# Talking-heads attention and a Fourier/FFN block on one core: moving the mixing stage's q, k and v loads to other steps

## The chip, the core and the metric

The kernel runs on one core of a Trainium2 chip. The metric is device time in microseconds (us) of one execution. Before the change the median of three runs is 2313.41 us (2312.7 to 2314.76). The profiled execution, from which every duration below is taken, is a separate one: it took 2319.37 us, and its first to last instruction span 2317.0 us.

The engines are named as in the profile: PE (matrix multiply), PEld (its weight load), DVE (vector), ACT (scalar), POOL (GpSimd), SP (the queue that issues most DMAs here). POOL computes and also issues DMAs; while it issues one, the rest of its queue waits.

## The reference, cut to what matters

```python
# q, k, v: (8 batches, 12 heads, 448, 64) fp32
scores = scale * np.matmul(q, k.transpose(0, 1, 3, 2))
scores = np.einsum('bhij,hg->bgij', scores, w_pre)      # mix the heads
attn = np.exp(scores - np.max(scores, axis=-1, keepdims=True))
attn = attn / (np.sum(attn, axis=-1, keepdims=True) + 1e-09)
attn = np.einsum('bhij,hg->bgij', attn, w_post)         # mix them again
x = np.matmul(attn, v)          # then (B, H, S, D) -> (B, S, H*D) = (8, 448, 768)
mixed = np.real(np.fft.fft(np.fft.fft(x, axis=1), axis=2))
u = x + mixed                   # then a layer norm over the last axis: un
ch = np.maximum(un @ w_ch1, 0.0) @ w_ch2                # 768 -> 3072 -> 768
out = u + ch
```

All of it is fp32.

## The kernel before, in words

There are two stages. `mix_phase` does the attention and the Fourier transform, batch after batch, and writes `u` to DRAM; `ffn_phase` does the norm and the two large products, with Strassen-like combinations of blocks. The change is in the first stage, which fills about the first 815 us of the profile.

**Steps.** The mixing stage is one software pipeline of 184 steps, 23 per batch (`GS`), and one step is about 4 us. A batch's 448 query rows are cut into 8 blocks of 2 or 3 steps (`BLOCKS`); a step handles 20 query rows of all 12 heads, laid out so that a small matrix product mixes the heads. For step T the work is spread over earlier steps: the block's q·k products (L628) are copied by ACT from PSUM to a tile `Sb` (L489, two buffers); at the end of step T-5 SP issues four gathers `Kr<-Sb` (L645, 105 KB each), which bring the rows of the 12 heads together; in step T-2 PE does the head mix `mx` (L656), DVE the row maximum (L663), ACT the exponential into `PP` (L670), and POOL divides by the row sums (L680, two instructions); in step T PE does the second head mix `po` (L690) and DVE transposes it (L703). The product with v (L720) comes after each group of two blocks.

A block's copy into `Sb` may not begin before the gathers of the block two before it have landed, because they read the same buffer. That is the wait `ACT Sb L489 <- DMA Kr<-Sb`.

**What else the steps carry.** Around this, each step carries work of the batch before or after: the transposes of the next batch's q and k (L601), the Fourier folds of the batch before on POOL (L785, L790, L799, L800, L806), its transforms on PE (L764, L829, L845), the sums `X` on DVE (L856, L858), the stores of `u` (L877 on SP, an indirect one at L868 and L874 on POOL), and one instruction per step of the preparation of the FFN's weights on DVE (L250 to L310), with its loads and stores on POOL (L234, L243).

**The order** is written by hand. Each piece of work has a due step (`due(kind, at, fn)`), and in every step `take` issues what is due. Pieces of kind "none", the loads among them, are issued first in their step. Within the step the engines' order follows `ORDERS`, of which there is one for even and one for odd steps; because a batch has 23 steps, a given step of a batch is even in one batch and odd in the next. PE, DVE, ACT and POOL execute in exactly the order written.

**The loads of q and k.** A batch needs six tiles, q and k for each of three groups of heads (`xx` = 0, 1, 2). They take turns in four buffers (`praw`). A tile is loaded in two halves (`y` = 0, 1), each half by two DMAs of 112 KB, and for all batches but the first POOL issues them (L572). The tiles are loaded in the order of their transposes, q0, k0, q2, q1, k2, k1, whose steps `AT_T` gives: 5, 9, 13, 15, 15 and 16 of the batch before. `AT_L` gives the steps in which the two halves of each of the six are issued, counted from the start of the batch before (so -4 is step 19 of the batch before that one); `AT_L1` is the same for batch 1. `AT_V` gives the steps for the two halves of the three v tiles, one DMA of 224 KB each (L581), counted in the batch that uses them; a v tile has one buffer, and its first half waits for the last product that reads the old one (steps 1, 3 and 4).

**The loads and the folds.** The two are tied together. `take` counts the halves of q and k that it issued, and after the scaling of a step

```python
if s < TOT - 3:
    for _ in range(min(len(folds), 1 if n and s > 3 else 2)):
        folds.pop(0)()
```

so one fold piece is issued in a step with such a load and two in a step without. Eight pieces become ready in step 0 of the next batch (popped from step 1), and twelve in its step 6 (popped from step 7). They come in the order pairs, pairs, sides, quarters for each of two combinations; the second list ends with four `both`. The transforms of step 16 (L829) need all of them.

Of the kernel before, what the change touches and what calls it, by code (L numbers as in the profile page):

```python
# [86 lines left out]


AT_T = ((5, 9), (15, 16), (13, 15))
AT_L = ((-4, -3), (-2, -1), (0, 1), (2, 7), (10, 11), (12, 13))  # L90
AT_V = ((2, 3), (4, 5), (6, 7))
AT_L1 = ((-12, -12), (-12, -12), (3, 4), (5, 6), (10, 11), (12, 13))
AT_QK0 = {2: (0, 1, 1), 3: (2, 3, 3), 4: (4, 5, 5)}
AT_QK = ((0, 2, 1), (0, 1, 2), (0, 1, 2), (1, 2, 2),
         (0, 1, 2), (0, 1, 2), (0, 1, 2), (0, 1, 2))
# [355 lines left out]
def mix_phase(ctx, tc, rest, ident, q, k, v, w_pre, w_post, u_scr, u_rev, wts, lead):  # L451
# [125 lines left out]
    def emit_load_v(b, pr, y):  # L577
        if y == 0:
            batches[b]["v", pr] = pvv.tile([P, 2, C7 * D], F32, name="vv", tag=f"vv{pr}")
        h = 6 * y + 2 * pr  # L580
        (nc.gpsimd if b else nc.sync).dma_start(  # L581
            out=batches[b]["v", pr][64 * y:64 * y + 64, :, :],
            in_=v[b, h:h + 2].rearrange("h (p c) d -> p h (c d)", c=C7))
# [301 lines left out]
    def due(kind, at, fn):  # L885
        fill[kind].append((at, len(fill[kind]), fn))
# [4 lines left out]
    for b in range(B):  # L891
# [14 lines left out]
        else:  # L906
            for at, (a, nm, xx) in zip(AT_L if b > 1 else AT_L1, sorted(at_t, key=lambda e: e[0])):
                for y in range(2):
# [6 lines left out]
        for pr in range(3 if b else 0):  # L915
            for y in range(2):
                due("none", f + AT_V[pr][y], lambda b=b, pr=pr, y=y: emit_load_v(b, pr, y))
        for n in range(0 if b else 2, NBL):
# [635 lines left out]
```

## Time and profile before

| | before |
|---|---|
| median of three runs | 2313.41 us |
| profiled execution: its own time / its span | 2319.37 / 2317.0 us |
| PE busy | 2260.0 us, 98% |
| DVE / ACT / POOL busy | 1719.4 / 1167.7 / 1292.1 us |
| mixing stage | up to about 815 us |
| batches 1 to 6 of it, each from its step 0 to the next one's | 93.4, 99.9, 99.3, 98.3, 100.7, 96.7 us |

Busy time of POOL takes in the DMAs that it issues; SP's issues are no busy time. A batch's start is read from the trace as the start of the first head-mix product (L656) of its step 0: 129.7, 223.1, 323.0, 422.3, 520.6, 621.3 and 718.0 us for batches 1 to 7. The start of any other step is read in the same way. Batches 2 to 6 do the same work, and batch 1 lacks only the last transforms of a batch two before it; so differences between them are waits. In the timeline a row is a run of like instructions: start, length, engine, line, tiles, count, and in brackets the idle time before it and what ended that.

### The profile page before, as it was taken

The numbers are of one execution on the slowest core, as the hardware profiler recorded it, in microseconds if no ns is written. First come the engines' busy times: TensorE is split into PE (matmuls) and PEld (weight loads), VectorE is DVE, ScalarE is ACT, GpSimd is POOL, SyncE is SP. The second block draws the span as 40 slices with busy tenths as digits, with TensorE's granted clock in tenths as the row PEclk, the third lists the DMA queues.
The fourth block names the chain that finished last, engine by engine and source line by source line (L and its number), as shares of the span: only waits on it lengthen the run. The fifth ranks groups of instructions, "written<-read, shape, count | busy, mean of one in ns | idle before, by whom it ended". The sixth has DMA issues, their size and how long they took to land.

```text
span 2317.0 us, 60784 instructions
## 1 busy us (share of the span) xinstructions
PE 2260.0 (98%) x22894; PEld 1743.0 (75%) x22894; DVE 1719.4 (74%) x3640; ACT 1167.7 (50%) x3330; POOL 1292.1 (56%) x1799
## 2 busy tenths in 40 slices
PE   7999999999999999999999999999999999999998
PEld 3455555555555577677899999999999999999998
DVE  4778778887877757787777787778777877865545
ACT  4776767666676632322354444444444445434434
POOL 5587968778787552121545465556545645444334
PEclk9999999999999999999999999999999999999999
DMA  7565655657666466567777887879877977795664
GB/s 167 163 185 165 184 168 163 193 157 187 181 178 194 139 233 217 187 218 271 204 180 211 202 239 204 207 178 261 212 168 197 287 169 183 194 246 124 146 147 76
DMA packets 228542, 439.44 MB, mean 190 GB/s; under 512 B 35964, under 2 KB 150326, under 8 KB 228252
## 3 DMA queue, kind: packets, MB, share of 16 engines
q1 hardware_dynamic: 157484, 302.90, 38.6%
q0 software_dynamic: 68480, 131.62, 30.5%
q8 instruction: 183, 3.00, 0.6%
q10 hardware_dynamic: 2288, 1.05, 0.2%
q14 instruction: 107, 0.88, 0.1%
HBM read 213.16 MB, written 143.16 MB: 154 GB/s over the span
## 4 chain that ended last, share of the span: by engine, by line
PE 88%; DVE 5%; DMA 3%; ACT 2%; issue 1%; POOL 1%; SPq 1%; DVEq 0%; ACTq 0%; POOLq 0%
PE psP L1213 18%; PE psP L1335 14%; PE psR L1213 9%; PE psR L1335 7%; PE mx L656 6%; PE ms L720 6%; PE ms L628 5%; PE po L690 5%; PE psQ L1213 4%; PE psQ L1335 3%; PE psP L1290 3%; PE ms L845 2%; PE ms L601 2%; DMA Kr<-Sb 1%; PE psR L1290 1%; PE ms L829 1%
## 5 line engine op out<-in xcount | busy, mean ns | idle before, releaser
L1369 POOL DMA_DIRECT2D out_dram<-od x172 | 208.9, 1277 | 262.6 <-DVE od L1357 171.9
L680 POOL TENSOR_SCALAR PP<-PP,rcp 128x448 f32<-128x448 f32 x368 | 235.3, 649 | 186.9 <-DVE rcp L678 144.0
L670 ACT ACTIVATE PP<-mx,nmx 128x448 f32<-128x448 f32 x368 | 230.2, 631 | 174.0 <-DVE nmx L663 155.7
L663 DVE TENSOR_REDUCE nmx<-mx 128x1 f32<-128x448 f32 x368 | 212.5, 617 | 103.9 <-PE mx L656 101.7
L1176 POOL TENSOR_TENSOR hq<-h 128x128 f32<-128x128 f32 (+1 forms) x210 | 130.0, 619 | 255.4 <-ACT h L1235 122.1
L1363 ACT COPY od<-psP 128x192 f32<-128x192 f32 x488 | 156.1, 320 | 172.4 <-PE psP L1335 171.0
L1366 DVE TENSOR_TENSOR od<-od 128x768 f32<-128x768 f32 x210 | 201.4, 972 | 52.8 <-ACT od L1363 52.4
L489 ACT COPY Sb<-ms 124x448 f32<-124x448 f32 (+1 forms) x378 | 181.7, 540 | 54.0 <-PE ms L628 23.5
L703 DVE STREAM_TRANSPOSE Pv<-po 128x896 f32<-128x896 f32 x184 | 203.5, 1106 | 4.6 <-PE po L690 3.7
L656 PE MATMUL mx<-Kr,kw 60*32 60x448 f32 x2944 | 199.0, 555 | 7.4 <-DMA Kr<-Sb 4.2
L628 PE MATMUL ms<-kT,qT 64*32 64x448 f32 (+1 forms) x3072 | 195.4, 544 | 9.0 <-ACT Sb L489 3.6
L720 PEld LDWEIGHTS ms<-Pv,vv 64*64 64x64 f32 x5376 | 137.9, 132 | 76.7 <-issue 46.4
L690 PE MATMUL po<-PP,kw 60*32 60x448 f32 x2944 | 187.8, 539 | 1.4 <-POOL PP L680 0.8
L1213 PE MATMUL psP<-qs,w1t 128*128 128x256 f32 x744 | 179.2, 379 | 1.4 <-DVE h L1234 1.4
L1213 PE MATMUL psP<-ks,w1t 128*128 128x256 f32 x744 | 179.2, 379 | 0.4 <-DVE h L1234 0.4
L720 PE MATMUL ms<-Pv,vv 64*64 64x120 f32 (+1 forms) x5376 | 160.7, 263 | 6.6 <-ACT Sb L489 3.5
L254 POOL TENSOR_SCALAR wst<-wst 128x256 f32<-128x256 f32 (+1 forms) x76 | 119.2, 1577 | 67.7 <-ACT wst L265 67.6
L1213 PEld LDWEIGHTS psP<-qs,w1t 128*128 128x128 f32 x744 | 139.3, 190 | 18.5 <-DVE h L1234 1.8
L1213 PEld LDWEIGHTS psP<-ks,w1t 128*128 128x128 f32 x744 | 139.3, 190 | 17.4 <-DVE h L1234 0.8
L1213 PE MATMUL psP<-ub,w1t 128*128 128x256 f32 x528 | 127.1, 379 | 0.3 <-DVE h L1234 0.3
L1234 DVE TENSOR_TENSOR h<-h,psP 128x512 f32<-128x512 f32 x42 | 28.8, 686 | 127.8 <-PE psP L1213 112.3
L1335 PE MATMUL psP<-w2t,hq 128*128 128x192 f32 x490 | 122.4, 332 | 1.2 <-DVE od L1357 1.2
(199 smaller groups left out, 5310.2 us busy)
## 6 DMA issues: line engine op xcount, KB each, us to landing
Kr<-Sb SPq DMA_DIRECT2D x730, 105.0 KB
out_dram<-od POOLq DMA_DIRECT2D x172, 384.0 KB, 6.6
qs<-ub SPq DMA_DIRECT2D x89, 384.0 KB
ks<-ub SPq DMA_DIRECT2D x88, 384.0 KB
ub<-ub SPq DMA_DIRECT2D x79, 384.0 KB
w1t<-w SPq DMA_DIRECT2D x42, 384.0 KB
w2t<-w SPq DMA_DIRECT2D x42, 384.0 KB
raw<-in_moe_w_ch_dram SPq DMA_DIRECT2D x32, 384.0 KB
```

The lines of the kernel that those rows point to most:

```text
L628: nc.tensor.matmul(pss[x][o:o + hi - lo, :S], st["qT", xx][64 * x:64 * x + 64, y, lo:hi], st["kT", xx][64 * x:64 * x + 64, y, :], start=Tr ...
L656: nc.tensor.matmul(mx[x][64 * z + o:64 * z + o + 32, :S], kw1[64 * x:64 * x + KR, o:o + 32], Kr[64 * x:64 * x + KR, z, :], start=True, sto ...
L663: nc.vector.tensor_reduce(nmx[:, :], steps[T]["mx"][x][:, :S], axis=AX.X, op=ALU.max, negate=True)
L670: nc.scalar.activation(steps[T]["PP"][:, x, :], steps[T]["mx"][x][:, :S], ACTF.Exp, bias=steps[T]["nmx", x][:, :], accum_out=steps[T]["den ...
L680: nc.gpsimd.tensor_scalar(PP[:, x, :], PP[:, x, :], rcp[:, x:x + 1], 1.0, op0=ALU.mult, op1=ALU.mult)
L690: nc.tensor.matmul(po[o:o + 32, z, :S], kw2[64 * z:64 * z + KR, y, :], PP[64 * z:64 * z + KR, :, c * HS:(c + 1) * HS], start=True, stop=True)
L703: nc.vector.transpose(turned[a]["Pv"][:, j, :].rearrange("p (z s) -> p z s", z=2), steps[T]["po"][:, :, :S])
L720: nc.tensor.matmul(pss[y][64 * x:64 * x + 64, :nu * R], st["v", pr][64 * y:64 * y + 64, x, jb * D:(jb + 1) * D], _ap(Pv, 64 * y * rp + 32 ...
L1213: mm = nc.tensor.matmul(p[:, m, :], w1[i][:, kc, m * P:(m + 1) * P], ub[:, kc, :], start=i in (0, 4, 1)[:3 - seed] and m == kc == 0, stop= ...
L1335: nc.tensor.matmul(ps[j, key][:, :DQ], a, b, start=m in (0, 4), stop=True, skip_group_check=True)
L1366: eng.tensor_tensor(D[j][:, :, :], D[j][:, :, :], D[k][:, :, :], op=ALU.add)
L1369: nc.gpsimd.dma_start(out=acc[t, r, d], in_=D[j][:, :, :], accum_op=ALU.add)
```

## The change

Three constants change. For batches 2 to 7 the first four tiles of q and k (q0, k0, q2, q1) are issued one half per step in steps 15 to 22 of the batch two before, where they were spread over steps 19 to 22 and then 0, 1, 2 and 7; k2 is issued in steps 8 and 9, where it was in 10 and 11; k1 stays in 12 and 13. For batch 1 three of its tiles are one or two steps sooner, within batch 0. Of v, the second half of the second tile goes from step 5 to 4, and the third tile from 6 and 7 to 5 and 6.

```diff
 AT_T = ((5, 9), (15, 16), (13, 15))
-AT_L = ((-4, -3), (-2, -1), (0, 1), (2, 7), (10, 11), (12, 13))
-AT_V = ((2, 3), (4, 5), (6, 7))
-AT_L1 = ((-12, -12), (-12, -12), (3, 4), (5, 6), (10, 11), (12, 13))
+AT_L = ((-8, -7), (-6, -5), (-4, -3), (-2, -1), (8, 9), (12, 13))
+AT_V = ((2, 3), (4, 4), (5, 6))
+AT_L1 = ((-12, -12), (-12, -12), (2, 3), (4, 5), (8, 9), (12, 13))
```

No instruction is added or taken away. The order on PE, DVE, ACT and SP is the same as before; on POOL the DMA issues and, through the rule above, the fold pieces stand elsewhere.

## The prediction

> **What bounds the kernel now.** I read the page's busy times first, then busy times by stretches of steps, then waits and timelines inside the stretches that are too long. PE is busy nearly throughout, so only its waits can be won or added:
>
> ```profile
> span 2317.0 us, 60784 instructions
> PE 2260.0 (98%) x22894; PEld 1743.0 (75%) x22894; DVE 1719.4 (74%) x3640; ACT 1167.7 (50%) x3330; POOL 1292.1 (56%) x1799
> ```
>
> PE is idle for 57 us of the whole span. The next view is the busy time in steps 0 to 3 of batches 2 to 6, one row each (the columns are named in the first line):
>
> ```profile
> core 0: us, PE busy (x) PEld busy (x) DVE busy (x) ACT busy (x) POOL busy (x), PEclk, DMA share, GB/s
> 223.10:243.10 20.00, 18.34 (x347) 9.84 (x343) 14.73 (x35) 11.60 (x38) 13.56 (x19) 1.00 0.74 207
> 323.00:344.80 21.80, 20.09 (x352) 10.55 (x348) 15.15 (x38) 12.06 (x41) 14.71 (x22) 0.92 0.82 215
> 422.30:440.60 18.30, 18.30 (x350) 10.23 (x350) 14.71 (x35) 11.59 (x38) 13.52 (x19) 1.00 0.81 217
> 520.60:542.80 22.20, 19.67 (x350) 10.45 (x346) 15.42 (x38) 12.19 (x41) 14.20 (x21) 0.92 0.82 192
> 621.30:639.10 17.80, 17.48 (x353) 9.72 (x352) 15.18 (x35) 11.65 (x37) 14.95 (x21) 1.00 0.77 207
> ```
>
> The same work takes 17.8 to 22.2 us. With the shortest as floor the excess is 100.1 - 5 x 17.8 = 11.1 us. The modelled ends of matmuls hide part of a wait in busy time, so I count lengths, not gaps. The same view of steps 15 to 18 gives 19.0, 16.9, 17.7, 17.3 and 16.8 us at a DMA share of 0.32 to 0.50: excess 87.7 - 5 x 16.8 = 3.7 us. Steps 19 to 22 take 16.7 us in all five batches: excess 0, with two q or k DMAs in every step. Steps 4 to 14, of which two batches stand here, give 44.2, 43.9, 45.6, 44.5 and 45.4 us, excess 223.6 - 5 x 43.9 = 4.1 us:
>
> ```profile
> 344.80:388.70 43.90, 43.44 (x972) 23.03 (x957) 35.79 (x71) 32.94 (x102) 43.05 (x67) 1.00 0.60 177
> 440.60:486.20 45.60, 44.02 (x964) 23.28 (x969) 38.37 (x75) 33.10 (x108) 44.12 (x68) 1.00 0.66 194
> ```
>
> Here POOL is the second full engine: 43.05 of 43.90 us and 44.12 of 45.60. So there are two different shortages, of DMA in steps 0 to 3 and of POOL in steps 4 to 14; in all 18.9 us.
>
> The timeline of batch 5, step 2, shows the first:
>
> ```profile
> 532.03 1.42 POOL L572 DMA_DIRECT2D rawq<-in_q_dram  x2
> 532.95 0.97 ACT L489 COPY Sb<-ms 124x448 f32<-124x448 f32 x2 [3.48 <-DMA Kr<-Sb]
> 533.54 1.41 PE L628 MATMUL ms<-kT,qT 64*32 64x448 f32 x16 [1.85 <-ACT Sb L489]
> ```
>
> ACT may not overwrite `Sb` until SP's gathers have landed, and PE waits for ACT. The gathers are late because the DMA engines are full: the q loads issued beside them take twice as long as in steps 19 to 22. The tile view of rawq, first for 520.6 to 536 us, then for 604.6 to 621 us:
>
> ```profile
> DMA to landing us min/median/max: 8.4/8.5/8.7
> ```
>
> ```profile
> DMA to landing us min/median/max: 4.4/4.4/4.4
> ```
>
> For the gathers I worked landings out of the trace's semaphore records (last record before the semaphore's next use). The slowest of a step's four takes a median of 7.0 to 7.3 us when issued in steps 0 to 2, and 2.4 to 3.4 us in 15 to 18. In step 0 it is 8.9, 8.0, 6.6, 8.8 and 4.3 us in batches 2 to 6; the long batches are those above 8.
>
> POOL's timeline, batch 4, shows the second shortage, an unbroken row:
>
> ```profile
> 471.96 1.49 POOL L572 DMA_DIRECT2D rawk<-in_k_dram  x2
> 473.49 1.25 POOL L680 TENSOR_SCALAR PP<-PP,rcp 128x448 f32<-128x448 f32 x2
> 474.71 0.99 POOL L785 TENSOR_TENSOR xs<-X 113x384 f32<-113x384 f32 x1
> 475.66 1.43 POOL L572 DMA_DIRECT2D rawk<-in_k_dram  x2
> ```
>
> There the scaling of `PP` ends 0.06 to 0.6 us before PE's `po` needs it in most of steps 8 to 15, against 4 us in steps 17 to 21 (worked out from the trace).
>
> **What the Trainium skill says.** "DMA: Bandwidth & Descriptors", section "SWDGE vs HWDGE vs iDMA": DMAs from POOL and from SP use the same DMA engines, which take turns between their queues. The landings above agree: loads on POOL and gathers on SP are slow together. The same page, "Anatomy of one DMA", fits 2.0 us plus bytes at 436 GB/s, an estimate of 2.3 us for 112 KB alone; the fastest q or k load of the trace took 2.9 us, so 8.5 us is mostly queueing. "SBUF — State Buffer", "SBUF: two separate sides": a POOL instruction and a DVE one that needs the second port exclude each other whole. The trace agrees: in batch 2, step 15, `tmp<-wst` (L289) took 3.06 us in place of 0.27 us while POOL ran without a pause, and PE then waited 1.05 us for DVE's `kT`.
>
> **The change part by part.**
>
> *q2 and the first half of q1 leave steps 0, 1 and 2.* That is 3 halves x 2 DMAs = 6. Their DMA cost from the windows: 19 to 22 (8 such DMAs, mean share 0.53) less 15 to 18 (none, mean 0.39) is 0.14 x 16.7 us / 8 = 0.29 us of all engines each; from packet times (one of 256 ns and one of 134 ns per engine) 0.39 us. So 6 x 0.29 to 0.39 = 1.7 to 2.3 us leave some 13 us, and the share there falls from about 0.8 to 0.62-0.67. v's loads, the stores of `u` and the weights stay. Steps 4 to 8 have a share of 0.7 and gathers of 4.2 to 4.7 us (6.7 in step 8), so I expect about 5 us, under the 6.6 that cost batch 4 little. I take two thirds of the 11.1 us: **-7.4 us**. Bounds: 0 if the rest keeps it full, -11.1 if all goes.
>
> *POOL in steps 0 to 15.* One issue is 0.722 us (tile rows). Eight leave steps 0 to 7 (5.8 us). The folds, with a pairs piece 1.0, sides 1.0, quarters 2 x 0.59 + 0.18 = 1.36, both 1.0 us, go two per step in steps 1 to 4, so the eight are done after step 4 rather than 5, and the twelve after 14 rather than 15. For steps 4 to 14: q1's second half -1.45, two pairs pieces now before step 4 -2.0, one `both` from step 15 +1.0, v unchanged but for -0.65 from its place at the edge; -2.5 to -3.1, so 43.4 us of work becomes about 40.6. I added POOL's work per step less the step's length for batch 4: the backlog peaked at 6 us in step 12 before (where about 4 are free) and peaks at 3.2 us after. That takes most of batch 4's excess (1.7 us in steps 4 to 14, 0.9 in 15 to 18) and some of batch 2's stretch at step 15, whose `both` piece is gone (2.2 us), say **-3 us**; bounds 0 and -6.
>
> *The loads come into steps 15 to 18.* Two DMAs a step, 1.45 us of POOL, which is busy 8.7 to 11.4 of 17 us there, and 4 x 2 x 0.29 to 0.39 = 2.3 to 3.1 us of DMA: the share goes from 0.39 to about 0.55, the value of steps 19 to 22, which lose nothing. **0**, covered by that slack; without it 0.2 to 1 us a batch. Steps 19 to 22 keep their number.
>
> *Waits of the moved loads.* q0's buffer is free after q2's transposes in step 13 (load in 15), k0's after q1's in 15 (load in 17), the others' after k2's and k1's in 15 and 16 (19, 21), k2's after q0's in 5 (load in 8). All are at least a step over, so the scaling of `PP` queued behind is not held. The loads land long before their transposes. **0**; were one late, POOL would hold the scaling, `po` and PE for a step, 4 us a batch.
>
> *k2 in steps 8 and 9, v a step sooner.* k2's four issues meet POOL with one fold per step in place of two: +1.45 and +0.45 us in the two steps, paid back in 9 and 10. Step 4 is POOL's worst: two v issues 1.3, scaling 1.25, the store 1.03, sides and quarters 2.36, in all 5.9 us in a 4.1 us step, backlog 2.6 us, inside the 4. v's third tile waits for a product of the step just before, as the second tile already does. DVE's stretched instruction at step 5 (four batches, 0.6 to 1 us each in steps 6 and 7) may come at step 4 instead. **0**, -3 to +3.
>
> *Batch 0.* Three tiles for batch 1 come one or two steps sooner, into the start-up, where `mx` waits for gathers as it is. **0**, +-1.5 us; steps 20 to 22 are unchanged there.
>
> Sum: -7.4 - 3 = -10.4 us on the profiled execution's 2319.37 us, so 2309.0. That execution is 6.0 us above the median of the runs. If that came out of the same waits, a third of the 18.9 us isn't there without the profiler; so I take three quarters: -7.9 us, 2313.4 - 7.9 = **2305.5 us**. After step 22 of the last batch the FFN stage, PE-bound, only starts sooner.
>
> **The rivals.**
>
> *The pile-up stays.* v (six DMAs of 224 KB), two stores of 336 KB and weights remain in steps 0 to 6, and batch 6 shows little stall at the same loads, so the excess may be their chance order. Then about 3 us: 2310.5. Against: the excess goes with the landing times.
>
> *All of it goes*, with batch 0's and 1's part too: 18.9 x 0.75 = 14 us or a little more: 2298.5. For: both shortages are relieved at once. Against: v and the stores.
>
> *The stall moves to step 18.* Block 1 of the next batch copies into `Sb` in step 18, behind gathers of step 17. Batch 0 shows the mechanism: in its steps 19 to 22 the tables are loaded beside q and k, gathers take 7 to 8 us, ACT waits 4.6 us for them in step 22, and the step is 2.7 us longer. In seven batches that is 19 us, less the 8 gained: +11, 2324. It decides once gathers of step 17 take over 7 us; they now take 2.4 to 4.9. Against: steps 19 to 22 carry these loads at 3.9 to 4.2 us without a loss.
>
> **How the numbers follow.** Forecast 0.52 (its own range 2300 to 2309), pile-up stays 0.22, all goes 0.16, stall moves 0.10. About 0.2% (4.6 us) is what a measurement of this kernel can tell from no change, so faster is below 2308.8 and slower above 2318.0. Faster: 0.52 and 0.16 and a little of the second, 0.70; same 0.20; slower 0.10. The range 2296 to 2316 leaves out the moved stall and the ends of the others.
>
> **What would show it.** Steps 0 to 3 of batches 2 to 6 sum to 91-94 us rather than 100.1, gathers of steps 0 to 2 land in 5 to 6 us, `ACT Sb <- DMA Kr` has no entry of over 2 us in batches 2 to 5; steps 4 to 14 lose 2 us and POOL has about 3 us of idle there; steps 15 to 22 don't grow. I am wrong if steps 0 to 3 keep gathers of 8 us, if POOL or the shared port stalls steps 4 and 5, or if steps 15 to 18 grow past 17.5 us.

## The result, and the profile after

| | before | after |
|---|---|---|
| median (six runs each) | 2314.54 us (2312.7 to 2317.01) | 2301.66 us (2298.69 to 2301.93) |
| profiled execution, its span | 2319.37 / 2317.0 us | 2301.93 / 2300.2 us |
| steps 0 to 3, batches 2 to 6 | 100.0 us | 89.5 us |
| steps 4 to 14, batches 2 to 6 | 223.7 us | 219.1 us |
| steps 15 to 18, batches 2 to 6 | 87.7 us | 85.2 us |
| steps 19 to 22, batches 2 to 6 | 83.6 us | 84.0 us |
| batches 0 and 1 | 92.3 and 93.4 us | 94.0 and 92.0 us |

The medians differ by 12.9 us. The ratio on record, which compares whole sets of runs and need not be exactly the quotient of the medians, is 0.9951 with a 95% interval of 0.994 to 0.9962, which is 8.8 to 13.9 us of 2314.5: a gain of half a per cent, clear of the noise. The profiled executions differ by more, 17.4 us, because the one of before lies 4.8 us above the median of its six runs. The stage lengths are read as in the prediction, from the first `mx` matmul of a step to that of another.

The page after, engines' busy times:

```profile
span 2300.2 us, 60788 instructions
PE 2250.3 (98%) x22894; PEld 1742.2 (76%) x22894; DVE 1710.8 (74%) x3640; ACT 1167.8 (51%) x3330; POOL 1287.1 (56%) x1799
```

The work is the same and the span is 16.8 us shorter; PE's idle time went from 57 to 50 us; the other 9.7 us are in PE's busy time, whose matmul ends are modelled. Busy times by stretch, steps 0 to 3 of batches 2 to 6:

```profile
core 0: us, PE busy (x) PEld busy (x) DVE busy (x) ACT busy (x) POOL busy (x), PEclk, DMA share, GB/s
221.60:239.70 18.10, 17.78 (x348) 9.77 (x343) 14.74 (x35) 11.65 (x38) 11.51 (x17) 1.00 0.61 183
316.90:335.20 18.30, 17.61 (x351) 9.77 (x345) 14.64 (x35) 11.61 (x39) 12.61 (x19) 1.00 0.68 199
413.40:431.10 17.70, 17.38 (x346) 9.77 (x342) 14.68 (x35) 11.66 (x38) 11.48 (x17) 1.00 0.65 182
509.20:526.90 17.70, 17.38 (x350) 9.61 (x342) 14.92 (x35) 11.76 (x39) 12.07 (x18) 1.00 0.64 190
604.00:621.70 17.70, 17.38 (x346) 9.67 (x342) 15.16 (x35) 11.64 (x38) 12.83 (x19) 1.00 0.64 190
```

The DMA share fell from 0.74-0.82 to 0.61-0.68, and three batches in a row take 17.7 us, the length of before's shortest: what waits are left there no longer lengthen it. Batch 5, step 2, where ACT had waited 3.48 us for the gathers and PE 1.85 us for ACT, in the timeline after:

```profile
518.47 0.97 ACT L489 COPY Sb<-ms 124x448 f32<-124x448 f32 x2 [0.42 <-DMA Kr<-Sb]
519.32 1.71 PE L628 MATMUL ms<-kT,qT 64*32 64x448 f32 x32
```

ACT's wait is 0.42 us and PE's is gone. The gathers of steps 0 to 3 (slowest of four, median of batches 1 to 6) land after 6.0, 4.8, 4.4 and 4.1 us, in place of 7.3, 7.0, 7.2 and 5.5. Of before two landing lines were shown, 8.4/8.5/8.7 us for the q loads beside the gathers and 4.4 for those in steps 19 to 22. After, q2 and q1 stand in steps 19 to 22 and land after 4.1 to 7.2 us in batch 5, median 4.4; and q0, which gave them its place, lands thus in steps 15 and 16 (tile view of rawq for 570 to 587 us):

```profile
DMA to landing us min/median/max: 3.9/4.0/4.1
```

Steps 4 to 14 of batches 3 and 4, the two that were shown of before:

```profile
335.20:378.70 43.50, 42.80 (x975) 22.73 (x967) 35.47 (x75) 33.30 (x106) 40.45 (x65) 1.00 0.58 179
431.10:475.30 44.20, 43.19 (x965) 22.80 (x967) 36.29 (x75) 33.26 (x109) 42.17 (x67) 1.00 0.66 197
```

POOL is busy for 40.45 and 42.17 us, 2 to 2.6 us less, and the stretches are 0.4 and 1.4 us shorter. POOL's timeline at the place in batch 4 (step 13 and 14) where its row had been unbroken:

```profile
470.66 1.43 POOL L572 DMA_DIRECT2D rawk<-in_k_dram  x2
472.13 1.25 POOL L680 TENSOR_SCALAR PP<-PP,rcp 128x448 f32<-128x448 f32 x2
473.35 1.01 POOL L806 TENSOR_TENSOR xf<-xq 113x385 f32<-113x385 f32 x1
474.31 0.10 POOL L595 MEMSET qT<- 128x8 f32 x1
474.35 0.10 POOL L596 MEMSET qT<- 128x10 f32 x1
475.19 1.40 POOL L680 TENSOR_SCALAR PP<-PP,rcp 128x448 f32<-128x448 f32 x2 [0.74 <-ACT XT L489]
```

POOL has a pause again before the scaling, which ends 1.4 to 3.3 us before PE's `po` in most of steps 8 to 15, where 0.06 to 0.6 us had been left.

Two places stand out as longer. In batch 3, step 15 takes 5.64 us in place of 4.47; the timeline there:

```profile
381.69 1.48 POOL L572 DMA_DIRECT2D rawq<-in_q_dram  x2
382.79 0.97 ACT L489 COPY Sb<-ms 124x448 f32<-124x448 f32 x2 [1.06 <-DMA Kr<-Sb]
383.38 0.98 PE L601 MATMUL ms<-ident,rawk 128*128 128x128 f32 x7 [1.32 <-ACT Sb L489]
```

It is the old wait, 1.06 us on ACT and 1.32 us on PE, beside a load that came into this step. One execution doesn't make it: step 15 of batch 3 takes 4.98 to 5.89 us in all nine profiled executions of this document that have loads there, and 4.47 or 4.48 in the three that have none. And batch 0 is 1.7 us longer in this execution, with a wait of 6.05 us for the gathers in its step 22, in place of 4.6; the slowest gathers issued in its steps 19 and 20 landed after 11.3 and 11.7 us, where before they took 8.8 and 8.2.

### The profile page after: what moved, and what is told of

Same layout as the page of the kernel before. It is cut to its first block, busy times and chain, and to the rows that moved or that the text cites. A ratio compares the mean times of both kernels' runs of the same rounds, so it can differ in the third digit from the quotient of the medians.

```text
span 2300.2 us, 60788 instructions
## 1 busy us (share of the span) xinstructions
PE 2250.3 (98%) x22894; PEld 1742.2 (76%) x22894; DVE 1710.8 (74%) x3640; ACT 1167.8 (51%) x3330; POOL 1287.1 (56%) x1799
## 5 line engine op out<-in xcount | busy, mean ns | idle before, releaser
L656 PE MATMUL mx<-Kr,kw 60*32 60x448 f32 x2944 | 193.9, 547 | 8.8 <-ACT PP L670 4.8
```

The source lines that it names most:

```text
L656: nc.tensor.matmul(mx[x][64 * z + o:64 * z + o + 32, :S], kw1[64 * x:64 * x + KR, o:o + 32], Kr[64 * x:64 * x + KR, z, :], start=True, sto ...
```

## The experiments

The theory: the q and k loads beside the gathers of steps 0 to 3 were the cost, and POOL's relief in steps 4 to 15 a smaller second. The rivals: that POOL's time counts and not the DMAs'; that only the fold pieces' new places count; and that k2, v and batch 1's tiles do part of it. All runs below were compared with runs of before on the same chip. Where this section gives the length of a stretch, it is that of the run's own profiled execution, summed over batches 2 to 6.

### The first four tiles alone

```diff
 # in before
-AT_L = ((-4, -3), (-2, -1), (0, 1), (2, 7), (10, 11), (12, 13))
+AT_L = ((-8, -7), (-6, -5), (-4, -3), (-2, -1), (10, 11), (12, 13))
```

> Before, with q0, k0, q2 and q1 alone moved to steps 15 to 22; k2, v and batch 1's loads where they were. Theory (the loads leave a full stretch, steps 0 to 3, and POOL's full steps 4 to 7): nearly all of the gain, 2302 to 2305 us, steps 0 to 3 of batches 2 to 6 sum to 92 us or less. Rival (k2, v and batch 1's tiles carry a good part): 2308 us or more.

Measured: 2303.0 us, ratio 0.9955 (0.9939 to 0.9971). Steps 0 to 3 take 90.8 us, 4 to 14 217.8 and 15 to 18 86.1. Nearly the whole gain is in these four tiles.

### The rest alone

```diff
 # in before: k2, v and batch 1's tiles as in after, the first four tiles as before
-AT_L = ((-4, -3), (-2, -1), (0, 1), (2, 7), (10, 11), (12, 13))
+AT_L = ((-4, -3), (-2, -1), (0, 1), (2, 7), (8, 9), (12, 13))
-AT_V = ((2, 3), (4, 5), (6, 7))
+AT_V = ((2, 3), (4, 4), (5, 6))
-AT_L1 = ((-12, -12), (-12, -12), (3, 4), (5, 6), (10, 11), (12, 13))
+AT_L1 = ((-12, -12), (-12, -12), (2, 3), (4, 5), (8, 9), (12, 13))
```

> The rest alone: k2 in steps 8 and 9, v and batch 1's tiles sooner, the first four tiles of batches 2 to 7 where they were. Theory: within 1.5 us of before, steps 0 to 3 still sum to 97 us or more. Rival: 4 us or more faster.

Measured: 2313.16 us, ratio 0.9995 (0.9984 to 1.0005). Steps 0 to 3 are at 101.9 us, 4 to 14 at 224.7, both as before. These edits are worth nothing by themselves, as the prediction had put them.

### After's loads with before's fold pieces

```diff
 # in after; FOLD_S: the steps in which before issues a half of q or k
-for _ in range(min(len(folds), 1 if n and s > 3 else 2)):
+for _ in range(min(len(folds), 1 if s in FOLD_S and s > 3 else 2)):
```

> After, with the fold pieces of POOL popped by the calendar of before (one in each step that had a q or k load before). Theory (DMA pile-up and POOL's issues, not the order of the folds): 2301 to 2305 us. Rival (the folds coming sooner make room on POOL): half of the gain is lost, 2307 us or more.

Measured: 2307.43 us, ratio 0.9966 (0.9955 to 0.9977). This is past the limit that the rival had named, though less than half of the gain is lost; the theory gave the folds too little. Steps 0 to 3 keep their gain (91.5 us). Steps 4 to 14 are back at 223.4 us, against 217.8 to 220.5 in the other eight profiled executions with the four tiles moved. Loads alone are worth about 7.9 us (0.34% of 2314.4), and the calendar of the folds some 3.5 to 5 more: 3.5 by the ratios, whose intervals overlap a little, 5.0 by the medians. Busy time by stretch, steps 4 to 14 of batches 3 and 4 of this kernel:

```profile
340.90:384.70 43.80, 43.34 (x967) 22.84 (x955) 36.95 (x75) 33.11 (x106) 42.43 (x68) 1.00 0.59 178
436.90:482.70 45.80, 44.13 (x966) 23.25 (x970) 38.53 (x75) 33.35 (x108) 43.96 (x70) 1.00 0.63 185
```

Batch 4 has POOL at 43.96 us again and is 45.8 us long, as before. Its timeline in step 5 shows what comes of it:

```profile
444.04 1.03 POOL L868 DMA_INDIRECT v<-X,rows  x1 [0.19 <-issue]
444.47 2.92 DVE L310 TENSOR_TENSOR wst<-wst 128x256 f32<-128x256 f32 x1
445.09 1.97 POOL L785 TENSOR_TENSOR xs<-X 113x384 f32<-113x384 f32 x2
447.32 1.08 DVE L489 COPY qT<-ms 128x512 f32<-128x512 f32 x1
448.46 0.91 PE L764 MATMUL ms<-ident,XT 128*113 128x128 f32 x6 [0.49 <-DVE qT L489]
```

DVE's weight preparation starts amid POOL's store and ends with POOL's two fold pieces, after 2.92 us; DVE's `qT` is queued behind it and PE waits 0.49 us. The Trainium skill names the lock in "SBUF — State Buffer", "SBUF: two separate sides": a DVE instruction with two SBUF inputs and a POOL one that reads SBUF exclude each other for a whole instruction. This instruction has two such inputs, and the trace agrees with the exclusion, but here the loser stood behind more than one instruction of the winner. Steps 6 and 7, right behind, take 4.23 and 4.63 us in this batch, against 3.26 and 4.04 in batch 4 after. Over batches 2 to 6 these two steps take 41.5 us here, 37.0 after and 39.3 before. These 4.5 us are as much as this kernel has lost to after in the whole of steps 4 to 14 (4.3).

The twelve profiled executions together bear this reading out. In twelve of the sixty batches 2 to 6 in them, four of before's among these, the longest weight instruction of step 5 lasted 1.7 us or more. In these, steps 6 and 7 together grow one for one with it: 7.70 us where it lasted 1.71, 8.09 at 2.14, 8.86 at 2.92. Where it lasted 1.3 us or less, they take 7.3 us in 39 of 48 cases and never more than 7.9. No run moved the weight preparation itself.

### Before's loads with after's fold pieces

```diff
 # in before; FOLD_S: the steps in which after issues a half of q or k
-for _ in range(min(len(folds), 1 if n and s > 3 else 2)):
+for _ in range(min(len(folds), 1 if s in FOLD_S and s > 3 else 2)):
```

> Before, with the fold pieces popped by the calendar of after, so that POOL has two pieces and the loads in steps 1 and 2. Theory: 2313 to 2318 us, no gain, as the loads are still in steps 0 to 3. Rival: 2309 us or less.

Measured: 2315.56 us, ratio 1.0008 (0.9994 to 1.0022): nothing. The fold calendar gains only once the loads are gone. The sums of steps 4 to 14, batches 2 to 6, first of this kernel, then of after:

```profile
sum 223.00, PE 217.09 PEld 115.84 DVE 187.62 ACT 166.35 POOL 205.62; mean PE 43.42 PEld 23.17 DVE 37.52 ACT 33.27 POOL 41.12
```

```profile
sum 219.20, PE 215.77 PEld 113.96 DVE 179.05 ACT 166.54 POOL 201.94; mean PE 43.15 PEld 22.79 DVE 35.81 ACT 33.31 POOL 40.39
```

Steps 0 to 3 take 96.4 us. In steps 4 to 14 POOL has 17.4 us to spare here too (223.0 - 205.6), and yet the stretch is no shorter than before's. So POOL's total doesn't set it. DVE's busy time does differ, 187.6 against 179.1 us for the same instructions. One place where it does, in the timeline of batch 5, step 8:

```profile
559.96 3.08 DVE L258 TENSOR_SCALAR wst<-tmp 128x384 uint32<-128x384 uint32 x1
560.62 1.24 POOL L680 TENSOR_SCALAR PP<-PP,rcp 128x448 f32<-128x448 f32 x2
561.83 0.99 POOL L790 TENSOR_TENSOR xs<-xs 113x383 f32<-113x383 f32 x1
563.67 0.64 ACT L670 ACTIVATE PP<-mx,nmx 128x448 f32<-128x448 f32 x1 [2.48 <-DVE nmx L663]
564.45 1.20 PE L656 MATMUL mx<-Kr,kw 60*32 60x448 f32 x12 [0.50 <-ACT PP L670]
```

The same instruction takes 0.34 us where POOL pauses (after, batch 4, at 487.37 us). Here it ends 0.2 us after POOL's row; the row maximum is late, ACT waits 2.48 us for it, and PE 0.50 us for ACT. This kernel has it in step 8 of batches 2, 3 and 5 (3.04, 2.96, 3.08 us), and its steps 9 and 10 take 3.3 us more than after's over the five batches (40.4 against 37.1). Another 1.9 us of the 4 by which its steps 4 to 14 are longer than after's lie in step 5 of batch 6, where PE stood still in the middle of a `po` for no wait that the trace shows. Before had a stretched instruction in step 5 of batches 2 to 5 (1.7 to 2.3 us) and in steps 10 and 15. After has at most 1.3 us in step 5, and about 2 us in step 4 of two batches, where nothing stands close behind.

### The loads put back, without taking anything away

```diff
 # in after, for batches 2 to 7: q2 and the first half of q1 are loaded a second time,
 # the same data into the tile that holds them, in the steps where before loaded them
+for nm, xx, y, a in (("q", 2, 0, 0), ("q", 2, 1, 1), ("q", 1, 0, 2)):
+    due("none", f - GS + a, lambda ...: emit_again(b, xx, nm, y))   # two DMAs of 112 KB on POOL
```

> After, with q2 (both halves) and the first half of q1 loaded a second time from the same data in steps 0, 1 and 2, into the tile that holds them already; folds as in after. Theory (DMA engines too full in steps 0 to 3): 6 to 10 us slower than after, 2308 to 2312 us, steps 0 to 3 of batches 2 to 6 back to 96 us or more. Rival (POOL's issue time and folds carry the gain): under 3 us slower.

Measured: 2311.13 us, ratio 0.9994 (0.9981 to 1.0008). Six DMAs of 112 KB per batch take the gain away in the medians. In the profiled execution steps 0 to 3 sum to 95.8 us, just short of the 96 that the theory had named: 6.3 of the 10.5 us are back. Batches 3 and 5:

```profile
321.70:341.70 20.00, 18.39 (x354) 9.77 (x349) 14.58 (x34) 11.56 (x39) 16.86 (x25) 1.00 0.83 213
515.10:535.30 20.20, 18.07 (x350) 9.63 (x342) 14.96 (x35) 11.69 (x39) 16.44 (x24) 1.00 0.78 199
```

The share is 0.83 and 0.78 again and the stretches 20 us. The repeated loads themselves, tile view of rawq for 515 to 532 us:

```profile
DMA to landing us min/median/max: 6.4/6.8/7.1
```

### POOL's time put back, without the transfers

```diff
 # in after, in the same places as the repeated loads
+for _ in range(5):
+    nc.gpsimd.memset(idle[:, :], 0.0)      # 128 x 256, 0.311 us each
```

> After, with five POOL memsets on an unused tile, about as long as two DMA issues, in steps 0, 1 and 2 in place of the second loads: POOL's time without the transfers. Theory (DMA): within 2 us of after in steps 0 to 3, at most 3 us slower in all, from POOL's backlog in steps 4 to 14. Rival (POOL): as slow as with the loads, 6 us or more.

Measured: 2301.69 us, ratio 0.9949 (0.9931 to 0.9967). By the ratios (0.9951 for after) it costs nothing. Steps 0 to 3 sum to 92.1 us, 2.6 more than in after and 1.9 more than in a second execution of after, so at the edge of the 2 that the theory allowed. The same two stretches as above:

```profile
321.40:341.00 19.60, 18.47 (x352) 9.83 (x346) 14.81 (x35) 11.63 (x39) 17.21 (x34) 1.00 0.63 186
514.40:532.70 18.30, 17.61 (x350) 9.66 (x342) 14.97 (x35) 11.62 (x38) 16.77 (x33) 1.00 0.63 183
```

POOL is as busy as with the loads (17.21 and 16.77 us against 16.86 and 16.44), the DMA share is 0.63. The two kernels, run side by side, differ by 9.4 us, and what differs is the transfers: in steps 0 to 2 they are what counts, and about the same POOL time without them is not. Batch 3 is not quite even in this, with 19.6 us at a share of 0.63; its gathers of step 0 landed after 7.0 us, and why they did one execution doesn't tell. The profiled executions show less than the medians, 5.5 us, 3.7 of it in steps 0 to 3.

Over all twelve profiled executions, steps 0 to 3 take 95.8 to 101.9 us in the four whose kernels load q there and 89.5 to 92.1 in the eight whose kernels do not, whatever the folds and POOL's time were.

### Batch 2's tiles as before, the tables elsewhere, and after again

The moved loads fall into the start-up for batch 2 alone, and in batch 0 the four table loads stand beside them. Three kernels look for something that the change loses there or elsewhere, and after was run again:

```diff
 # in after: the first four tiles of batch 2 alone as in before
+AT_L2 = ((-4, -3), (-2, -1), (0, 1), (2, 7), (8, 9), (12, 13))      # b == 2
```

> After, with batch 2's first four tiles alone on the calendar of before, so that batch 0 has no loads in steps 15 to 18. Theory (meeting of loads and tables): 1 to 4 us faster than after, batch 0 at 92 us. Rival (chance): within 1.5 us of after.

```diff
 # in after: the tables loaded in batch 1
-for at, t in ((9, rows), (16, ts), (17, tcs first half), (19, tcs second half)):
+for at, t in ((33, rows), (33, ts), (34, tcs first half), (37, tcs second half)):
```

> After, with the tables of the Fourier transform (rows, ts, tcs; batch 0, steps 9 to 19) loaded in batch 1, steps 10, 10, 11 and 14. Theory (batch 0 pays for the change where the moved loads meet the tables, ACT waiting 6.05 us for gathers in its step 22): 2 to 5 us faster than after, 2297 to 2300 us, batch 0 under 91 us. Rival (batch 0's length is the start-up's chance): within 1.5 us of after.

```diff
 # in after: the tables at 30, 32, 33, 34, and the FFN's first four loads four steps sooner
-due("none", f - 4 + 2 * x + y, lambda x=x, y=y: lead.load(x, y))
+due("none", f - 8 + 2 * x + y, lambda x=x, y=y: lead.load(x, y))
```

> After, with the tables in batch 1, steps 7, 9, 10 and 11, and the FFN stage's eight first loads of u four steps sooner (steps 15 to 22 of batch 6 in place of 19 to 22 and 0 to 3 of batch 7). Theory (the same two moves where loads still meet a full stretch): 4 to 7 us faster than after, 2295 to 2298 us. Rival (what is left is chance): within 2 us of after.

The last is after unchanged, beside the one above on the same chip:

> After once more, unchanged, beside the combined version: 2300 to 2303 us, 0.4 to 0.6% under before; it gives the base for the differences of a few us, and a second trace of the same program, whose stalls in steps 0 to 3 should sum to 89 to 92 us again.

Measured, as ratios to before: batch 2 as before 0.9945 (0.9927 to 0.9962), tables in batch 1 0.9943 (0.9924 to 0.9962), tables and first FFN loads 0.9946 (0.9928 to 0.9964), after again 0.9947 (0.9929 to 0.9965). The last two, run side by side, are 2298.74 and 2299.75 us: 1.0 us apart, where the theory had 4 to 7 and the rival under 2. The first two had no run of after beside them. All four lie inside the interval of after, so no better version can be named, and gains of 1 to 4 us are neither shown nor excluded. After again is 9.0 us under the median of before measured beside it (2308.73), a little faster than expected in itself and with the ratio as expected; its steps 0 to 3 sum to 90.2 us, as expected.

The traces show something in batch 0. Where batch 2's first loads stand in its steps 15 to 18 beside the tables, it takes 94.0 to 98.9 us (six executions); without those loads 90.0 to 94.6 (four); with the loads and the tables in batch 1, 88.9 and 89.7. Part of the last comes back, as batch 1 grows from 92.0 to 94.3 and 95.0 us. What is left is too small for the medians to show.

## Why the prediction was right, and where its sizes were off

**Direction and main mechanism: right.** The forecast was 2305.5 us, the measured median 2301.66. It lies in the range and in the likeliest case's own range (2300 to 2309), but in size it is nearer to the rival *all of it goes* (2298.5), which had a chance of 0.16. What was to show it did: steps 0 to 3 sum to 89.5 us (91 to 94 foreseen), the DMA share is 0.61 to 0.68 (0.62 to 0.67), no wait `ACT Sb <- DMA Kr` of over 2 us is left in this execution. ACT's waits on DMAs from batch 2 to step 3 of batch 6 (us in total, times, longest), first before, then after:

```profile
ACT X L489 <- DMA u<-X: 7.0, 3, 3.9
ACT Sb L489 <- DMA Kr<-Sb: 5.9, 3, 3.5
```

```profile
ACT X L489 <- DMA u<-X: 3.8, 3, 1.9
ACT Sb L489 <- DMA Kr<-Sb: 2.8, 3, 1.3
```

The first row is a wait of the same kind that the prediction did not name: ACT may not overwrite `X` before a store of `u` has read it. Its longest, 3.85 us, is in batch 2 of before (the copy at 230.91 us), at the place where that batch lost 2.3 us. So the gathers were not all of the pile-up's cost. The moved loads are only a part of this wait: over the twelve profiled executions its longest is 2.5 to 3.9 us with them in steps 0 to 3, and 1.4 to 2.9 without.

**-7.4 us for q2 and q1 leaving steps 0 to 2: undersized.** The profile lost 10.5 us there. The landing estimate of about 5 us was good (6.0, 4.8, 4.4, 4.1); the step that failed is "I take two thirds of the 11.1 us". In step 0 of batches 2 to 6 of after the gathers land after 6.2, 6.4, 6.0, 5.9 and 4.2 us and little is lost, so the cost doesn't fall in proportion to the landing time. A gather is hidden until it outlasts the time to the next copy into its buffer. The twelve profiled executions together show where that was for step 2 of batches 3, 5 and 7: while the gathers issued in step 0 landed within 6.2 us, step 2 took 5.03 us (six cases); beyond 6.3 us it was longer in all 28 cases, by about one us for each us or more: 5.25 at 6.55, 6.0 at 7.3, 8.89 at 8.84. In batches 2, 4 and 6, whose steps follow the other of the two `ORDERS`, step 2 took 5.05 to 5.25 us with gathers of up to 8.9 us. That the order makes this difference is not tested. The 6.6 us "that cost batch 4 little" came from a batch of the second kind.

**-3 us for POOL in steps 4 to 18: undersized, and worked out from the wrong wait.** The profile lost 4.6 us in steps 4 to 14 and 2.5 in 15 to 18. POOL got 3.5 us of idle per batch (17.3 us in five), where about 3 was foreseen. But the backlog before `PP` that the sum was worked out from was tight in batch 4 alone (in steps 8 to 15 of batches 3, 5 and 6 of before about 1 us or more was left), and before's loads with after's folds had as much idle and no gain. Of the 4.6 us, 2.3 lie in steps 6 and 7 (39.3 to 37.0 us), behind the DVE weight instruction of step 5 that stands behind an unbroken row of POOL and delays `qT`. The other 2.3 were no shortage of POOL but late gathers again: 1.3 in step 4 of batch 6, where before's copy into `Sb` began 0.14 us after a gather of step 2 had landed, and 1.0 in step 10 of batches 3 and 5, where before's ACT waited 1.04 and 1.41 us for gathers of step 8. The 2.5 us in steps 15 to 18 lie in batches 2 and 4 (2.2 and 0.9, where before had weight instructions of 3.06 and 1.74 us) and 5 (0.5), less a loss of 1.2 in batch 3.

**0 for the loads in steps 15 to 18: nearly right.** Together these steps are shorter, but batch 3 pays 1.2 us in step 15 and, at 18.1 us, passes the 17.5 that was to mean wrong. The DMA share there rose to 0.57, 0.57, 0.63 and 0.72 in batches 2 to 5, where about 0.55 was foreseen. The share is not what decided: batch 5 lost nothing at 0.72 and batch 3 lost 1.2 us at 0.57.

**0 for the moved waits, for k2 and v, and for batch 0.** The second experiment measured k2, v and batch 1's tiles as nothing. No scaling of `PP` was held by a late buffer. Batch 0 was undersized: by the means of the executions counted above the traces have it some 3 us longer where the moved loads meet the tables (95.8 against 92.4 us), twice what was allowed. Under batch 0 the prediction counted batch 1's tiles alone and left out batch 2's loads, which come into its steps 15 to 18.

**Scaling by three quarters: close, in part by luck.** The profiled executions differ by 17.4 us and the medians by 12.9, a ratio of 0.74; with the second execution of after and the medians measured beside it, it is 0.61 (14.8 and 9.0 us). Unprofiled runs of before reach 2323 us, so its profiled 2319.37 is within their spread, and no cost of the profiler is shown. Of the 17.4, 17.2 lie in batches 2 to 6; batches 0, 1 and the rest cancel. What the scaling was applied to, 10.4, was 7 us short (three quarters of it are 7.8, not 7.9).

**The rivals.** *The pile-up stays* is out: v, the stores and the weights remain and don't stall at a share of 0.65. *All of it goes* was close in the trace (17.2 of 18.9 us), and its 2298.5 us is 3.2 from the measured median, against 3.8 for the forecast. *The stall moves to step 18* is out, and so is its deciding point. In batch 4 the gathers that SP issued in steps 16 to 18 took 7.7, 8.6 and 7.5 us beside weights and q loads, over the 7 us, and the steps took 4.13, 4.14 and 4.06. The next copies into `Sb` and the PE row behind them, timeline of batch 4, step 19:

```profile
494.30 0.97 ACT L489 COPY Sb<-ms 124x448 f32<-124x448 f32 x2 [2.30 <-PE po L690]
494.89 1.02 PE L829 MATMUL ms<-ts,xf 112*96 112x113 f32 x8 [0.32 <-ACT Sb L489]
```

ACT was idle for 2.30 us ahead of the copy (the `po` named had ended 0.5 us before it), but PE had other work and waited 0.32 us; step 19 took 5.04 us where the other batches take 4.65 or 4.67. In step 22 of batch 0 a wait of 6.05 us left 1.29 us on PE. So the landing time at which PE stalls isn't one number for all steps; it depends on what is written between the copy and PE's next need of it.

## What to carry to other kernels

Look for background loads beside transfers that something waits for, and for a stretch with a lower DMA share to put them in. The test of a stretch is not its share alone but whether the latency-bound transfers in it land before the next writer of their buffer needs them: in the steps measured here more load cost next to nothing up to that point, and past it about each microsecond was PE's. When a queue issues both loads and compute, a load that is moved moves the compute too; separate the two in an experiment (the loads with the old order, the order with the old loads, the transfers without the issue time), because here they gained about 8 us and nothing alone, and 11 to 13 us together. Before a forecast is taken from one profiled execution, compare it with the median: before's lay 4.8 us above its own, after's 0.3, and of what the traces differ by only 0.61 and 0.74 is in the medians.

## What the runs showed of the hardware that had not been expected

- A DVE instruction can stand behind several POOL instructions in a row: 3.08 us in place of 0.34 through the rest of a fold, two scalings and another fold, and 2.92 us in place of 0.40 through the issue of an indirect store and two folds.
- Six more DMAs of 112 KB in some 12 us, with stores and v's loads beside them, land in 6.4 to 7.1 us (batch 5) and cost 9.4 us over six batches, while about the same POOL time without a transfer costs nothing that can be measured.
- Four loads of 112 KB landed in 3.9 to 4.1 us in a stretch of DMA share 0.72 (after, batch 5, steps 15 to 18), where six took 8.4 to 8.7 at 0.82 (before, batch 5, steps 0 to 3): the share alone does not tell the landing time.
- Gathers of 8.6 us cost 0.4 us in one place (batch 4, issued in step 17), where gathers of 8 to 9 us in step 0 of before stood in stretches that were 2.2 to 4.4 us too long.
